# Attention and two MoE layers in float32: the products with V of two heads written into the two partition halves of one bank, and row sums from key blocks added up beforehand

## The chip, the cores and the metric

One core of one Trainium2 chip runs one program. The metric is the device time of one execution in microseconds, the median of three runs. The profile is one execution taken by the hardware profiler. Its engines are TensorE (PE for matmuls, PEld for weight loads), VectorE (DVE), ScalarE (ACT), GpSimd (POOL) and the DMA queue that SyncE (SP) issues.

## What is computed

Causal attention for 2 batches of 12 heads, 448 positions, 64 elements per head, and then two feed-forward layers on the 896 tokens. The part that the change touches is the attention:

```python
scores = scale * np.matmul(q, k.transpose(0, 1, 3, 2))
scores = np.where(mask, -1000000000.0, scores)
scores = scores - np.max(scores, axis=-1, keepdims=True)
attn = np.exp(scores)
attn = attn / (np.sum(attn, axis=-1, keepdims=True) + 1e-09)
return np.matmul(attn, v).astype(np.float32)
```

Its result (896 tokens of 768) goes through `h = x @ w_in` (1024 wide), a gated softmax, a layer norm, `@ w_out`, and then `relu(x @ w_in2)**2 @ w_out2` (2048 wide).

## The kernel before

The 24 heads are worked in 12 pairs. A pair's K and Q lie with head 0 on partitions 0 to 63 and head 1 on partitions 64 to 127. Per pair i the steps are, by the names of the table `SEQ` and with the lines of the profile:

- `H`, `L`: K and Q are split into a rounded part (ACT, L242) and a rest (DVE, L246; pair 0 on POOL). `S0a` to `S0c`, `mxa` to `mxc`: a first product of scores (L257) whose row maximum DVE takes out of PSUM against the mask (L272); `mT`, `row`, `rowd` bring the maxima into a row (L284, L289, L301, L302).
- `Sa`, `Sb` (L317, L325): the scores, transposed, so that partitions are keys and columns are queries, in two PSUM tiles of two banks, one bank per head. Half a holds key block 0 (queries 0 to 447, in columns 64 to 511) and key block 3 (queries 384 to 447, in columns 0 to 63); half b holds key block 1 (queries 128 to 447, columns 192 to 511) and key block 2 (queries 256 to 447, columns 0 to 191). The products of the two heads use the two row halves of the array.
- `ea1`, `eb1` (ACT, L349): the exponential into a buffer `PP` in SBUF, of which there are five. `ka`, `kb` (POOL, L346): the causal mask on the diagonal blocks.
- `Ua`, `Ub` (PE, L358): the products with V in float32, for each head two key blocks per half. The weights are 128 wide: 64 columns of V and 64 columns of ones (buffer `VR`, set to ones at L231), so that partitions 0 to 63 of the bank of a head receive the unnormalised output and partitions 64 to 127 the row sum.
- `E` (ACT, L369) takes the two banks to SBUF in one instruction and adds the 1e-9; `sums` (L374), `recips` (DVE, L380), `rcd` (L386) and `spread` (L392) bring the row sums into 112 lanes, take reciprocals, and broadcast them through DRAM into the one buffer `bc`. `norm` (POOL, L399) multiplies, one instruction of 64 partitions per head; `x_hi` (ACT, L407) and `x_lo` (DVE, L411) split the result for the next matmuls.

`h` (L474) are the matmuls of the first layer; each needs the `x` parts of a pair and a converted block of `w_in` (`wf`, `wh`, `wl`, L149 to L151, L465, L469). The order on every engine is that of `SEQ`, written out by hand: each engine runs its share of the table in that order, and an instruction that waits holds up all that stand behind it on its engine. SP issues the DMAs in the same way. Eight PSUM banks are handed out as four tiles of two banks; `bank2` takes one and `give` returns it. From about 94 us on the first `h` matmuls are mixed with the last products with V.

Of the kernel before, what the change touches and what calls it, by code (L numbers as in the profile page):

```python
# [29 lines left out]
row.1 mxb.2 ka.0 rowd.1 L.2 lq.1 S0a.2 S0c.2 Ua.0 mxa.2 H.3 load_r.4 eb1.0 mxc.2 S0a.3 kb.0 mT.2 mxa.3 Sa.1 row.2 lq.2  # L30
rowd.2 L.3 S0c.3 Ub.0 ea1.1 load_r.5 mxc.3 ka.1 S0b.3 E.0 Sb.1 mxb.3 sums.0 Sa.2 H.4 eb1.1 mT.3 L.4 Sb.2 load_r.6
row.3 lq.3 ea1.2 kb.1 recips.0 S0b.4 rowd.3 Ua.1 mxb.4 H.5 rcd.0 eb1.2 L.5 lq.8 S0c.4 lq.5 S0a.5 S0a.4 kb.2 mxc.4
load_v.2 Ub.1 mxa.4 ka.2 spread.0 mT.4 E.1 Sa.3 wf.0 row.4 sums.1 Sb.3 ea1.3 rowd.4 S0b.5 H.6 Ua.2 load_v.3 norm.0
mxa.5 eb1.3 load_r.7 wh.0 recips.1 S0c.5 mxb.5 Ub.2 rcd.1 ld.3 kb.3 mxc.5 E.2 wl.0 mT.5 Sa.4 row.5 sums.2 x_hi.0 L.6
rowd.5 ea1.4 S0a.6 Sb.4 ka.3 mxa.6 lq.6 S0c.6 spread.1 ka.4 eb1.4 S0b.6 mxc.6 Ua.3 load_r.8 mxb.6 H.7 kb.4 S0b.7
x_lo.0 mT.6 lq.7 Sa.5 L.7 row.6 load_v.4 rowd.6 norm.1 recips.2 S0a.7 ea1.5 mxb.7 Ub.3 rcd.2 load_r.9 mxa.7 S0c.7 Sb.5
ka.5 x_hi.1 mxc.7 load_v.5 Sa.6 x_lo.1 eb1.5 spread.2 wf.1 E.3 mT.7 Sb.6 ea1.6 sums.3 Ua.4 lq.9 row.7 load_r.10 H.8
norm.2 S0b.8 eb1.6 recips.3 S0a.8 mxb.8 Ub.4 rcd.3 wh.1 rowd.7 kb.5 mxa.8 S0c.8 load_v.6 E.4 Ua.5 mxc.8 ka.6 spread.3
x_hi.2 sums.4 H.9 L.8 mT.8 Sa.7 row.8 x_lo.2 load_r.11 L.9 rowd.8 Sb.7 ea1.7 norm.3 recips.4 S0b.9 rcd.4 H.10 S0a.9
Ub.5 load_v.7 mxa.9 eb1.7 lq.10 mxb.9 kb.6 x_hi.3 S0c.9 Sa.8 spread.4 E.5 mxc.9 kb.7 S0a.10 sums.5 ea1.8 mT.9 mxa.10  # L40
Sb.8 ka.7 row.9 lq.11 S0c.10 rowd.9 Ua.6 x_lo.3 L.10 norm.4 recips.5 S0b.10 rcd.5 eb1.8 Ub.6 mxb.10 load_v.8 load_g.0
mxc.10 ka.8 Sa.9 x_hi.4 spread.5 E.6 x_lo.4 Ua.7 H.11 wf.2 sums.6 ld.4 ea1.9 mT.10 Sb.9 row.10 rowd.10 S0a.11 eb1.9
recips.6 kb.8 Ua.8 mxa.11 rcd.6 load_v.9 norm.5 S0b.11 S0c.11 Ub.7 mxb.11 ka.9 x_hi.5 mxc.11 spread.6 Sa.10 E.7 x_lo.5
wl.1 mT.11 Ua.9 row.11 ea1.10 rowd.11 L.11 kb.9 sums.7 Sb.10 norm.6 Ub.8 eb1.10 recips.7 rcd.7 Sa.11 wf.3 load_v.10
E.8 Ub.9 x_hi.6 sums.8 wh.2 spread.7 Sb.11 ea1.11 x_lo.6 wh.3 h0.0 recips.8 wl.2 rcd.8 eb1.11 h0.1 norm.7 h1.0 ka.11
h1.1 x_hi.7 E.9 x_lo.7 h2.0 wl.3 sums.9 spread.8 load_v.11 h0.2 ka.10 kb.10 h2.1 recips.9 rcd.9 wf.4 ld.5 h1.2 Ua.10
norm.8 h0.3 Ub.10 kb.11 x_hi.8 spread.9 wh.4 x_lo.8 h2.2 E.10 wf.5 sums.10 h1.3 Ua.11 wl.4 wh.5 norm.9 recips.10 Ub.11
rcd.10 h1.4 wl.5 E.11 spread.10 h0.4 x_hi.9 sums.11 x_lo.9 h0.5 h1.5 norm.10 recips.11 mx.0 rcd.11 h2.3 mx.1 x_hi.10
h2.4 ex.0 spread.11 x_lo.10 h2.5 ex.1 mu.0 h3.0 mu.1 sq.0 norm.11 h3.1 de.0 sq.1 mx.2 h3.2 va.0 x_hi.11 pw.0 ex.2 h3.3
x_lo.11 fa.0 lw.0 ln.0 mu.2 h3.4 de.1 sq.2 h3.5 de.2 va.2 T.0 mx.3 pw.2 h4.0 Th.0 lw.1 ex.3 Tl.0 h4.1 va.1 h4.2 mu.3  # L50
pw.1 h4.3 fa.1 sq.3 fa.2 de.3 of.0 h4.4 ln.2 lw.2 ln.1 h4.5 of.1 oh.0 T.1 h5.0 mx.4 h5.1 lw.3 va.3 ex.4 h5.2 ol.0 pw.3
oh.1 fa.3 h5.3 mu.4 Th.1 h5.4 of.2 sq.4 h5.5 lw.4 ol.1 h6.0 oh.2 mx.5 T.2 Tl.1 h6.1 ex.5 of.3 Th.2 h6.2 lw.5 l2.0 ln.3
h6.3 mu.5 oh.3 T.3 h6.4 Tl.2 Th.3 sq.5 Tl.3 h6.5 lw.6 l2.1 de.5 y0.0 ol.2 l2.2 de.4 va.5 ol.3 va.4 y0.1 mx.6 pw.4 pw.5
# [784 lines left out]
```

## Time and profile before

| | |
|---|---|
| median of 3 runs | 459.95 us (459.81 to 460.13) |
| span of the profiled execution | 459.8 us, first to last instruction |
| PE busy | 452.7 us (98%) |
| weight loads (PEld) | 402.0 us (87%) |
| DVE busy | 275.1 us (60%) |
| ACT busy | 164.6 us (36%) |
| POOL busy | 120.8 us (26%) |
| products with V (L358) | 192 matmul records, 49.2 us of busy time |
| chain that ended last | PE 93%, of which the products with V 9% |

A program matmul on float32 (not on the rounded kind) stands in the trace as two records, each with its own weight load: 96 such products with V are 192 records. Busy times of PE overlap, since matmuls are pipelined; the chain that ended last gives each piece the time from its start to the next piece. The profiled execution's own time is its span and a little before the first and after the last instruction; the median of the runs is 0.15 us above the span. The products with V end at about 116 us; from 52 us on every piece of the chain that ended last is PE's, but for a few hundredths of a us and the last copy.

### The profile page before, as it was taken

The numbers are of one execution on the slowest core, as the hardware profiler recorded it, in microseconds if no ns is written. First come the engines' busy times: TensorE is split into PE (matmuls) and PEld (weight loads), VectorE is DVE, ScalarE is ACT, GpSimd is POOL, SyncE is SP. The second block draws the span as 40 slices with busy tenths as digits, with TensorE's granted clock in tenths as the row PEclk, the third lists the DMA queues.
The fourth block names the chain that finished last, engine by engine and source line by source line (L and its number), as shares of the span: only waits on it lengthen the run. The fifth ranks groups of instructions, "written<-read, shape, count | busy, mean of one in ns | idle before, by whom it ended". The sixth has DMA issues, their size and how long they took to land.

```text
span 459.8 us, 6525 instructions
## 1 busy us (share of the span) xinstructions
PE 452.7 (98%) x2535; PEld 402.0 (87%) x2535; DVE 275.1 (60%) x524; ACT 164.6 (36%) x213; POOL 120.8 (26%) x122
## 2 busy tenths in 40 slices
...
GB/s 251 128 154 221 207 159 164 62 79 98 41 280 133 96 248 2 0 1 0 0 138 69 138 80 127 116 91 137 70 137 80 128 113 94 240 90 135 86 52 120
DMA packets 41689, 52.47 MB, mean 114 GB/s; under 512 B 18234, under 2 KB 32314, under 8 KB 41274
## 3 DMA queue, kind: packets, MB, share of 16 engines
...
HBM read 49.16 MB, written 2.80 MB: 113 GB/s over the span
## 4 chain that ended last, share of the span: by engine, by line
PE 93%; DMA 1%; POOL 1%; ACT 0%; issue 0%; SPq 0%; ACTq 0%; POOLq 0%
PE h L752 25%; PE o L781 25%; PE y L621 13%; PE h L474 13%; PE U L358 9%; PE s L317 4%; PE mxp L257 1%; DMA bc<-d 1%; PE T L599 1%; PE s L325 1%; POOL x L399 1%; PE mxp L284 0%; PE s L333 0%; ACT PP L349 0%; SPq L301 0%
## 5 line engine op out<-in xcount | busy, mean ns | idle before, releaser
L752 PE MATMUL h<-yT,w 128*128 128x448 f32 x576 | 116.9, 365 | 0.0
L781 PE MATMUL o<-w,g 128*128 128x384 f32 x672 | 116.8, 336 | 0.0
L781 PEld LDWEIGHTS o<-w,g 128*128 128x128 f32 x672 | 116.5, 188 | 0.3 <-DVE relu L738 0.2
L752 PEld LDWEIGHTS h<-yT,w 128*128 128x128 f32 x576 | 108.2, 188 | 8.6
L677 POOL TENSOR_TENSOR w<-wf,w 128x768 fp32r<-128x768 f32 x32 | 59.4, 1856 | 206.2 <-ACT w L674 206.2
L149 DVE TENSOR_SCALAR wf<-raw 128x768 int32<-128x768 int32 (+1 forms) x46 | 26.3, 573 | 83.6 <-DMA raw<-in_moe_w_out_dram 58.2
L674 ACT CAST w<-wf 128x768 fp32r<-128x768 f32 x32 | 26.8, 838 | 137.7 <-DVE wf L151 99.4
L474 PE MATMUL h<-w,xT 128*128 128x512 f32 x252 | 59.5, 393 | 0.0
L621 PE MATMUL y<-lnT,w 128*128 128x384 f32 (+1 forms) x288 | 58.9, 365 | 0.0
L621 PEld LDWEIGHTS y<-lnT,w 128*128 128x128 f32 x288 | 51.9, 188 | 5.9
L474 PEld LDWEIGHTS h<-w,xT 128*128 128x128 f32 x252 | 46.8, 188 | 9.6
L358 PE MATMUL U<-PP,VR 128*128 128x448 f32 (+1 forms) x192 | 49.2, 400 | 0.1
L151 DVE SCALAR_TENSOR_TENSOR wf<-raw,wf 128x768 int32<-128x768 int32 (+1 forms) x46 | 47.3, 1029 | 1.6
L150 DVE SCALAR_TENSOR_TENSOR wf<-raw,wf 128x768 int32<-128x768 int32 (+1 forms) x46 | 47.2, 1027 | 1.6
L358 PEld LDWEIGHTS U<-PP,VR 128*128 128x128 f32 x192 | 32.1, 190 | 16.4 <-issue 11.1
L399 POOL TENSOR_TENSOR x<-E,bc 64x448 f32<-64x448 f32 x24 | 31.9, 1328 | 47.2 <-DMA bc<-d 42.7
L272 DVE CUSTOM_DVE_ANT_0 JK<-mxp,MK 112x336 bf16<-112x336 f32 (+2 forms) x96 | 38.8, 446 | 8.5 <-PE mxp L257 7.5
L349 ACT ACTIVATE PP<-s 128x1024 f32<-128x1024 f32 x24 | 24.5, 1023 | 12.9 <-PE s L325 7.2
L738 DVE TENSOR_TENSOR relu<-h,relu 128x896 f32<-128x896 f32 x16 | 17.5, 1092 | 14.6 <-ACT relu L737 14.6
L346 POOL TENSOR_SCALAR_AFFINE_SELECT PP<-PP 128x256 f32<-128x256 f32 (+1 forms) x48 | 19.7, 443 | 21.3 <-ACT PP L349 20.8
L740 ACT CAST g<-relu 128x896 fp32r<-128x896 f32 x16 | 15.1, 942 | 18.6 <-DVE relu L738 18.6
L650 DVE TENSOR_TENSOR yT<-y,yT 128x384 fp32r<-128x384 f32 (+1 forms) x12 | 7.4, 624 | 22.7 <-ACT yT L649 22.7
...
## 6 DMA issues: line engine op xcount, KB each, us to landing
...
```

The lines of the kernel that those rows point to most:

```text
L149: nc.vector.tensor_scalar(xi, hw, 3, 0x3FFFFFFF, ALU.logical_shift_left, ALU.bitwise_and)
L150: nc.vector.scalar_tensor_tensor(xi, hw, -0x40000000, xi, ALU.bitwise_and, ALU.bitwise_or)
L151: nc.vector.scalar_tensor_tensor(xi, lw, 29, xi, ALU.logical_shift_right, ALU.bitwise_or)
L272: nc.vector.tensor_tensor_reduce(JK[t], b[0:JP, h, o : o + nk], MK[:, S - nk :], 1.0, NEG, ALU.add, ALU.max, mx[i][:, 4 * h + t : 4 * h + ...
L358: nc.tensor.matmul(UB[i][:, h, q0:S], VR[i % 3][:, t, h, :], PP[(2 * i + a) % NPP][:, h, o : o + nq], start=t == 0, stop=t == 2,)
L399: nc.gpsimd.tensor_tensor(x[D * h : D * h + D], e[0:D, h], bc[:, h], ALU.mult)
L474: nc.tensor.matmul(b[:, half, :], xT[c][s][:, t * P : t * P + P], W1[c][:, w, 512 * half : 512 * half + 512], start=(c == 0 and s == 0 and ...
L621: nc.tensor.matmul(b[:, ci, 0:n], WO[fi][:, w, c * P : c * P + P], M["lnT"][a][s][:, fi, :], start=(fi == 0 and w == 0 and s == 0), stop=( ...
L674: nc.scalar.copy(W2[n][:, 0], w_f["2", n])
L677: nc.gpsimd.tensor_tensor(W2[n][:, 1], w_f["2", n], f(W2[n][:, 0]), ALU.subtract)
L752: nc.tensor.matmul(b[:, a, 0:HT], W2[fi][:, w, c * P : c * P + P], yT[c][s][:, HT * a : HT * a + HT], start=(c == 0 and w == 0 and s == 0) ...
L781: nc.tensor.matmul(ob, G[fi + e][s][:, P * t : P * t + P], w, start=(fi + e == 0 and r == 0), stop=(fi + e == NF2 - 1 and r == 2),)
```

## The change

A pair's products with V take weights of 64 columns (V alone). Head 0 writes partitions 0 to 63 and head 1 partitions 64 to 127 of one bank, and the two heads' matmuls of one key block now stand next to each other. The row sums come from elsewhere: a new step `ad` (`row_add`, POOL) adds the key blocks of queries 128 to 447 into a tile `ps`, in three instructions, and a new step `Us` (`row_sum`, PE) multiplies by 64 columns of ones, once the 128 queries that only key block 0 reaches, and once `ps`, into the second bank of the same PSUM tile. `E` becomes two instructions, `sums` and `spread` two DMAs each, `norm` one instruction on 128 partitions. V is loaded into a buffer without gaps, the memsets of the ones in it go, and there are six `PP` buffers in place of five. In the table `ad.i` stands behind the later of `ka.i` and `kb.i`, and `Us.i` behind `Ub.i`; nothing else in its order changes.

```diff
-NPP = 5
+NPP = 6
...
-            VR = [per.tile([P, 4, 2, 2 * D], F32, name=f"VR{i}") for i in range(3)]
+            VR = [per.tile([P, 4, 2, D], F32, name=f"VR{i}") for i in range(3)]
+            ONES = per.tile([P, D], F32, name="ONES")
...
+            Q2 = S - P
...
-                nc.sync.dma_start(VR[i % 3][:, :, :, 0:D], v[i])
+                nc.sync.dma_start(VR[i % 3], v[i])
...
-            for i in range(3):
-                nc.vector.memset(VR[i][:, :, :, D:], 1.0)
+            nc.vector.memset(ONES, 1.0)
...
-                for h in range(2):
-                    for t, o, q0, nq in HALF[a]:
+                for t, o, q0, nq in HALF[a]:
+                    for h in range(2):
                         nc.tensor.matmul(
-                            UB[i][:, h, q0:S],
+                            UB[i][D * h : D * h + D, 0, q0:S],
                             VR[i % 3][:, t, h, :],
                             PP[(2 * i + a) % NPP][:, h, o : o + nq],
                             start=t == 0,
                             stop=t == 2,
                         )
 
+            def row_add(i):
+
+                pa, pb = (PP[(2 * i + a) % NPP] for a in range(2))
+                ps[i] = p = lat.tile([P, 2, Q2], F32, tag="ps", name="ps", bufs=2)
+                nc.gpsimd.tensor_tensor(p, pa[:, :, 512 - Q2 :], pb[:, :, 512 - Q2 :], ALU.add)
+                for o, x in ((P, pb[:, :, 0 : Q2 - P]), (2 * P, pa[:, :, 0 : Q2 - 2 * P])):
+                    nc.gpsimd.tensor_tensor(p[:, :, o:], p[:, :, o:], x, ALU.add)
+
+            def row_sum(i):
+
+                p, pa = ps.pop(i), PP[(2 * i) % NPP]
+                for o, x in ((0, pa[:, :, D : D + P]), (P, p)):
+                    n = x.shape[2]
+                    for h in range(2):
+                        nc.tensor.matmul(
+                            UB[i][D * h : D * h + D, 1, o : o + n], ONES, x[:, h], start=o == 0, stop=o > 0
+                        )
+
             def u_out(i):
...
-                nc.scalar.activation(ee[i], U[:, :, 0:S], AF.Identity, bias=SE)
+                nc.scalar.activation(ee[i][0 : D + 1, 1], U[0 : D + 1, 1, 0:S], AF.Identity, bias=SE[0 : D + 1])
+                nc.scalar.copy(ee[i][:, 0], U[:, 0, 0:S])
...
-                nc.sync.dma_start(c, ee[i][D : D + 1].rearrange("o h s -> o (h s)").rearrange("o (p j) -> o p j", j=8))
+                for h in range(2):
+                    r = ee[i][D * h : D * h + 1, 1].rearrange("o (p j) -> o p j", j=8)
+                    nc.sync.dma_start(c[JP // 2 * h : JP // 2 * h + JP // 2], r)
...
-                bc = lat.tile([D, 2, S], F32, tag="bc", name="bc", bufs=1)
-                nc.sync.dma_start(bc, d.rearrange("(h s) -> h s", h=2).unsqueeze(0).broadcast_to((D, 2, S)))
+                bc = lat.tile([P, S], F32, tag="bc", name="bc", bufs=1)
+                for h in range(2):
+                    nc.sync.dma_start(
+                        bc[D * h : D * h + D], d[S * h : S * h + S].unsqueeze(0).broadcast_to((D, S))
+                    )
...
-                for h in range(2):
-                    nc.gpsimd.tensor_tensor(x[D * h : D * h + D], e[0:D, h], bc[:, h], ALU.mult)
+                nc.gpsimd.tensor_tensor(x, e[:, 0], bc, ALU.mult)
```

The order on PE, at the second half of pair 0 (`PP_139` and `VR_135` are its exponentials and V, `HI_118` the keys and queries of pair 3, whose products for the row maximum stand around it), before:

```order
L257 MATMUL mxp<-HI_118 128x224 x2
L358 MATMUL U<-PP_139,VR_135 128x320
L358 MATMUL U<-PP_139,VR_135 128x192
L358 MATMUL U<-PP_139,VR_135 128x320
L358 MATMUL U<-PP_139,VR_135 128x192
L257 MATMUL mxp<-HI_118 128x336 x2
```

and now (the second half's exponentials are `PP_140` here, the first half's `PP_139`):

```order
L259 MATMUL mxp<-HI_118 128x224 x2
L360 MATMUL U<-PP_140,VR_135 64x320 x2
L360 MATMUL U<-PP_140,VR_135 64x192 x2
L382 MATMUL U<-PP_139,ONES 64x128 x2
L382 MATMUL U<-ps,ONES 64x320 x2
L259 MATMUL mxp<-HI_118 128x336 x2
```

The two heads of a key block stand side by side (x2), each 64 columns of weights wide, and four matmuls with the ones follow; of these the last two read `ps`.

The order on POOL, from the masks of pair 1 to the first `norm` (`PP_140`, `PP_141` are the halves of pair 1 before, `PP_138` and `PP_142` those of pair 2), before:

```order
L346 AFFINE_SELECT PP_140<-PP_140 128x2x64
L346 AFFINE_SELECT PP_140<-PP_140 128x2x128
L346 AFFINE_SELECT PP_141<-PP_141 128x2x128 x2
L346 AFFINE_SELECT PP_138<-PP_138 128x2x128 x2
L346 AFFINE_SELECT PP_142<-PP_142 128x2x64
L346 AFFINE_SELECT PP_142<-PP_142 128x2x128
L399 TENSOR_TENSOR x<-E,bc 64x448 x2
```

and now (pair 1 has `PP_141` and `PP_142`, pair 2 `PP_143` and `PP_144`):

```order
L348 AFFINE_SELECT PP_142<-PP_142 128x2x128 x2
L372 TENSOR_TENSOR ps<-PP_141,PP_142 128x640
L374 TENSOR_TENSOR ps<-ps,PP_142 128x2x192
L374 TENSOR_TENSOR ps<-ps,PP_141 128x2x64
L348 AFFINE_SELECT PP_144<-PP_144 128x2x128 x2
L348 AFFINE_SELECT PP_143<-PP_143 128x2x64
L348 AFFINE_SELECT PP_143<-PP_143 128x2x128
L372 TENSOR_TENSOR ps<-PP_143,PP_144 128x640
L374 TENSOR_TENSOR ps<-ps,PP_144 128x2x192
L374 TENSOR_TENSOR ps<-ps,PP_143 128x2x64
L424 TENSOR_TENSOR x<-E,bc 128x448
```

Three additions stand behind the masks of every pair, ahead of the masks of the next pair and of `norm`, and `norm` is one instruction.

## Rows read from the trace of the kernel before

**Rows 1.** Stages: stretch, us, busy PE PEld DVE ACT POOL, clock, DMA share, GB/s.
```profile
12.00:38.00 26.00, 25.57 (x198) 19.22 (x198) 22.57 (x79) 14.88 (x19) 8.91 (x18) 1.00 0.53 156
38.00:52.00 14.00, 12.43 (x113) 9.42 (x110) 10.67 (x39) 7.25 (x11) 5.02 (x9) 1.00 0.86 230
52.00:93.00 41.00, 40.93 (x292) 29.76 (x292) 33.18 (x90) 25.55 (x34) 20.27 (x28) 1.00 0.50 134
93.00:117.00 24.00, 24.00 (x114) 18.94 (x111) 13.72 (x14) 7.26 (x9) 12.77 (x14) 1.00 0.29 81
```
**Rows 2.** The chain that ended last, in order of time (start, length, what).
```profile
15.82 2.09 PE U L358 x8
...
29.18 1.93 PE U L358 x8
...
41.72 6.12 DMA bc<-d
...
47.98 1.16 POOL x L399
...
49.21 1.15 POOL x L399
...
51.92 1.02 PE s L317 x10
...
104.77 1.89 PE U L358 x8
...
108.11 1.73 PE U L358 x8
...
112.59 3.68 PE U L358 x16
```
**Rows 3.** Weight loads in one `Ua` (start, length, records): they follow the matmuls.
```profile
54.59 0.19 PEld L358 LDWEIGHTS U<-PP,VR 128*128 128x128 f32 x1 [0.19 <-issue]
54.97 0.19 PEld L358 LDWEIGHTS U<-PP,VR 128*128 128x128 f32 x1 [0.19 <-issue]
```
**Rows 4.** Groups of PE by form (count, busy us, mean ns).
```profile
L358 PE MATMUL U<-PP,VR 128*128 128x448 f32 x48 | 23.5, 571 | 0.1
...
L325 PE MATMUL s<-MR,NEG 64*128 64x512 f32 x22 | 5.2, 472 | 0.0
```
**Rows 5.** PE in order of time: one pair of 64-row matmuls.
```profile
61.26 0.48 PE L325 MATMUL s<-MR,NEG 64*128 64x512 f32 x2
```
**Rows 6.** Single lines of POOL and DVE: ns min/median/max.
```profile
L399 POOL TENSOR_TENSOR x<-E,bc x24: 1125/1155/2024, 33.8 to 126.0; 64x448 f32<-64x448 f32 x24
L677 POOL TENSOR_TENSOR w<-wf,w x32: 1842/1852/1942, 193.2 to 442.7; 128x768 fp32r<-128x768 f32 x32
L246 DVE TENSOR_TENSOR LO<-r,HI x11: 1084/1089/2024, 12.5 to 84.2; 128x896 fp32r<-128x896 f32 x11
```
**Rows 7.** POOL in order of time: masks of pairs 0 to 2.
```profile
16.45 0.77 POOL L346 TENSOR_SCALAR_AFFINE_SELECT PP<-PP 128x256 f32<-128x256 f32 x2 [2.38 <-ACT PP L349]
...
25.32 0.77 POOL L346 TENSOR_SCALAR_AFFINE_SELECT PP<-PP 128x256 f32<-128x256 f32 x2 [3.67 <-ACT PP L349]
28.10 1.89 POOL L346 TENSOR_SCALAR_AFFINE_SELECT PP<-PP 128x256 f32<-128x256 f32 x4 [2.01 <-ACT PP L349]
```
**Rows 8.** PE in order of time: `Ub` of pairs 0 and 1.
```profile
20.10 2.00 PE L358 MATMUL U<-PP,VR 128*128 128x320 f32 x8
...
29.11 2.00 PE L358 MATMUL U<-PP,VR 128*128 128x320 f32 x8
```
**Rows 9.** ACT and SP lines that `E`, `sums` and `spread` touch: ns min/median/max.
```profile
L369 ACT ACTIVATE E<-U,SE x12: 1003/1011/1014, 22.1 to 116.4; 128x896 f32<-128x896 f32 x12
L407 ACT CAST xT<-x x12: 549/564/567, 39.4 to 127.4; 128x448 fp32r<-128x448 f32 x12
L374 SPq DMA_DIRECT2D sc<-E x12: 532/564/609, 23.2 to 117.5; - x12
L392 SPq DMA_DIRECT2D bc<-d x12: 453/490/606, 28.7 to 121.2; - x12
```

More of the change, by code (lines that the diff above doesn't have):

```diff
@@ L29 @@
 load_v.0 lq.4 S0a.1 mxr.0 S0c.1 lq.0 fl.8 mxc.1 S0b.1 Sa.0 mxa.1 mxb.1 H.2 load_r.3 L.1 ea1.0 load_v.1 mT.1 S0b.2 Sb.0
[L30 to L53, printed above, removed]
@@ L54 @@
-of.4 lw.7 y0.2 of.5 oh.4 ex.6 y0.3 fa.4 oh.5 ol.4 de.6 mu.6 y0.4 of.6 sq.6 ln.4 ol.5 oh.6 T.4 fa.5 va.6 y0.5 Th.4 ol.6
-pw.6 ln.5 fa.6 Tl.4 ln.6 of.7 T.5 y0.6 Th.5 Tl.5 oh.7 ol.7 T.6 y0.7 Th.6 Tl.6 f2.0 y1.0 yo.0 f2.1 g2.0 o2.0 y1.1 yp.0
-g2.1 yo.2 o2.1 yo.1 y1.2 yp.1 yp.2
+row.1 mxb.2 ka.0 rowd.1 L.2 lq.1 S0a.2 S0c.2 Ua.0 mxa.2 H.3 load_r.4 eb1.0 mxc.2 S0a.3 kb.0 ad.0 mT.2 mxa.3 Sa.1 row.2
+lq.2 rowd.2 L.3 S0c.3 Ub.0 Us.0 ea1.1 load_r.5 mxc.3 ka.1 S0b.3 E.0 Sb.1 mxb.3 sums.0 Sa.2 H.4 eb1.1 mT.3 L.4 Sb.2
@@ new lines @@
+load_r.6 row.3 lq.3 ea1.2 kb.1 ad.1 recips.0 S0b.4 rowd.3 Ua.1 mxb.4 H.5 rcd.0 eb1.2 L.5 lq.8 S0c.4 lq.5 S0a.5 S0a.4
+kb.2 mxc.4 load_v.2 Ub.1 Us.1 mxa.4 ka.2 ad.2 spread.0 mT.4 E.1 Sa.3 wf.0 row.4 sums.1 Sb.3 ea1.3 rowd.4 S0b.5 H.6
+Ua.2 load_v.3 norm.0 mxa.5 eb1.3 load_r.7 wh.0 recips.1 S0c.5 mxb.5 Ub.2 Us.2 rcd.1 ld.3 kb.3 mxc.5 E.2 wl.0 mT.5 Sa.4
+row.5 sums.2 x_hi.0 L.6 rowd.5 ea1.4 S0a.6 Sb.4 ka.3 ad.3 mxa.6 lq.6 S0c.6 spread.1 ka.4 eb1.4 S0b.6 mxc.6 Ua.3
+load_r.8 mxb.6 H.7 kb.4 ad.4 S0b.7 x_lo.0 mT.6 lq.7 Sa.5 L.7 row.6 load_v.4 rowd.6 norm.1 recips.2 S0a.7 ea1.5 mxb.7
@@ new lines @@
+Ub.3 Us.3 rcd.2 load_r.9 mxa.7 S0c.7 Sb.5 ka.5 x_hi.1 mxc.7 load_v.5 Sa.6 x_lo.1 eb1.5 spread.2 wf.1 E.3 mT.7 Sb.6
+ea1.6 sums.3 Ua.4 lq.9 row.7 load_r.10 H.8 norm.2 S0b.8 eb1.6 recips.3 S0a.8 mxb.8 Ub.4 Us.4 rcd.3 wh.1 rowd.7 kb.5
+ad.5 mxa.8 S0c.8 load_v.6 E.4 Ua.5 mxc.8 ka.6 spread.3 x_hi.2 sums.4 H.9 L.8 mT.8 Sa.7 row.8 x_lo.2 load_r.11 L.9
+rowd.8 Sb.7 ea1.7 norm.3 recips.4 S0b.9 rcd.4 H.10 S0a.9 Ub.5 Us.5 load_v.7 mxa.9 eb1.7 lq.10 mxb.9 kb.6 ad.6 x_hi.3
+S0c.9 Sa.8 spread.4 E.5 mxc.9 kb.7 S0a.10 sums.5 ea1.8 mT.9 mxa.10 Sb.8 ka.7 ad.7 row.9 lq.11 S0c.10 rowd.9 Ua.6
@@ new lines @@
+x_lo.3 L.10 norm.4 recips.5 S0b.10 rcd.5 eb1.8 Ub.6 Us.6 mxb.10 load_v.8 load_g.0 mxc.10 ka.8 Sa.9 x_hi.4 spread.5 E.6
+x_lo.4 Ua.7 H.11 wf.2 sums.6 ld.4 ea1.9 mT.10 Sb.9 row.10 rowd.10 S0a.11 eb1.9 recips.6 kb.8 ad.8 Ua.8 mxa.11 rcd.6
+load_v.9 norm.5 S0b.11 S0c.11 Ub.7 Us.7 mxb.11 ka.9 x_hi.5 mxc.11 spread.6 Sa.10 E.7 x_lo.5 wl.1 mT.11 Ua.9 row.11
+ea1.10 rowd.11 L.11 kb.9 ad.9 sums.7 Sb.10 norm.6 Ub.8 Us.8 eb1.10 recips.7 rcd.7 Sa.11 wf.3 load_v.10 E.8 Ub.9 Us.9
+x_hi.6 sums.8 wh.2 spread.7 Sb.11 ea1.11 x_lo.6 wh.3 h0.0 recips.8 wl.2 rcd.8 eb1.11 h0.1 norm.7 h1.0 ka.11 h1.1
```

17 lines of the change are left out of this document (15 added, 2 removed).

## The prediction

> **What bounds the kernel now.** I read the stages first, then the chain that ended last, then the rows of the instructions that the change touches. The stages [rows 1] show PE with next to no gap from 12 us on, but for 38 to 52 us, where 1.6 of 14 us are empty. DVE is the next engine: 22.6 of 26 us up to 38 us, 33.2 of 41 us from 52 to 93 us. POOL has room: 8.9 of 26 us, 5.0 of 14, 20.3 of 41, 12.8 of 24. The chain [rows 2] runs through PE, and 22 of the 24 blocks of products with V are in it, at 1.9 to 2.1 us each, from 15.82 to 116.27 us (the two of pair 3 are not). Between 38 and 52 us it leaves PE: the broadcast of pair 1's reciprocals takes 6.12 us, `norm` on POOL 1.16 and 1.15 us, and only then the exponential comes that releases PE at 51.92 us. So a shorter block of products counts in eleven pairs, and a shorter `norm` once.
>
> **Price of a pass.** A float32 product stands in the trace as two passes: 48 records for 24 products of 448 columns [rows 4]. Two such passes follow each other 0.38 us apart, 54.59 to 54.97 us [rows 3], that is 0.85 ns a column: 0.27 us for 320 columns, 0.16 for 192, 0.11 for 128, 0.054 for 64. `Ua` is four passes of 448 and four of 64, 1.74 us; `Ub` four of 320 and four of 192, 1.74 us; a pair 3.48 us. The blocks in the chain take 0.2 to 0.35 us more [rows 2], for coming in and going out, which stays.
>
> **The products with V after the change.** The passes are as many and as long, since their time goes by the columns that stream, but each fills half the array's columns. `Us` adds four passes of 128 and four of 320 per pair, 1.52 us. All depends on how far the two heads' passes lie on each other. The trace of before has no product with 64 columns of weights. Nearest are the products of 64 rows: two of 512 columns lie within 0.48 us [rows 5], where one takes 0.47 us [rows 4], so two halves of the array do work at once. Each of these is a single pass, though, and the two halves alternate. Here the order is: head 0 first pass, head 0 second pass, head 1 first, head 1 second. I take it that a pass starts no earlier than the one issued before it, as all rows of PE that I read have it. Then head 0's first pass runs alone, its second beside head 1's first, and head 1's second beside the next short passes of head 0. `Ua` becomes three passes of 448 and two of 64: 1.25 us, 0.49 less. `Ub` and `Us` together become 3 x 0.27 + 2 x 0.16 (`Ub`), 2 x 0.11 (head 1's products of 128), and 0.70 us more, since head 0's first pass over `ps` lies beside the second of these: 2.06 us, 0.32 more than `Ub` alone. A pair gains 0.17 us, eleven pairs **1.9 us**. The bounds are no overlap, 1.52 us a pair more (+16.7 us), and full overlap, (3.48 + 1.52) / 2 = 2.50 us, 0.98 a pair less (-10.8 us). The value taken is nearest to the row of the 64-row pairs, with the order of the passes laid over it. The Trainium skill, TensorE: Matmul & The Clock Gate, Part 3, says that matmuls start and end strictly in program order, and that only weight loads are pulled ahead; by that rule the staggered sum above stands, and no row here shows it for two passes on one half.
>
> **Change of shape.** Among the `h` products, of the same 128 by 128 shape, the two kinds of block take 1.89 and 1.73 us instead of 2.09 and 1.93 [rows 2]: 0.2 us less than among products of 64 rows. With 64 columns they lose this. There are three such blocks (`Ua.10`; `Ub.10` with `Us.10`; pair 11 in one): **+0.6 us**. Everywhere else the shape changes at the same places as before.
>
> **The stretch from 38 to 52 us.** `norm` becomes one instruction of 128 partitions and 448 columns; I take the columns to set its time, so the second 1.15 us and the handover of 0.07 go [rows 2]: -1.2 us. `E` is two instructions of about 0.56 us (as the copies of `x_hi`, [rows 9]) instead of one of 1.01: +0.1. The second `sums` costs SP 0.56 us, but the first may go 0.45 us earlier, when the first half of `E` is done: +0.1. The second `spread` is issued 0.49 us after the first [rows 9], and `norm` needs both: 0 to 0.5, taken as 0.4, since each half is half the bytes. Behind these on SP stand the loads of Q, K and V, which wait for buffers anyway. Sum **-0.6 us**. That V arrives without gaps helps the queue by an amount I can't price; I take nothing. Exponentials that wait for a sixth buffer are off the chain, and so are the memsets, for the first row maximum waits for PE.
>
> **POOL.** An addition of 448 columns takes 1.125 us at least, one of 768 columns 1.842 us [rows 6]: 2.24 ns a column and 0.12 us. The three of `ad` (640, 384 and 128 columns) take 1.55, 0.98 and 0.41 us, with two handovers of 0.07 us 3.1 us a pair, 37 us in all, less 12 x 1.2 us of `norm`. That fits the gaps of each stage: about 18 of 26 us, 10 of 14, 30 of 41. What counts is when `ps` is ready. Pair 0's masks end at 17.22 us and pair 1's at 26.09 us [rows 7], so `ps` is there at 20.3 and 29.2 us. `Ub` starts at 20.10 and 29.11 us [rows 8], sooner by what has been gained up to there (0.49 and 0.66 us), and `Us` asks for `ps` 1.25 us later: 20.85 and 29.70 us. Half a us is spare in each; from pair 2 on more. Behind `ad.1` the masks of pair 2 wait from 28.1 to 29.2 us [rows 7]; their products come after those of pair 1 and two blocks of scores, so nobody waits for that. `ad` before `norm` costs nothing while `norm` waits for the broadcast, as its masks do now. Waits for `ps`: 0 to 1.2 us, taken as **+0.3**. What POOL and DVE do to each other: `norm` took 1.125 us at best and 2.02 at worst, DVE's subtraction L246 1.08 and 2.02 us [rows 6], so a single collision costs about 0.93 us; for pairs 0 to 4 that is 0 to 4.7 us, taken as **+0.5**, as medians are near the minima today.
>
> **Sum.** -1.9 + 0.6 - 0.6 + 0.3 + 0.5 = -1.1 us against the profiled execution, 459.8 us of span and 0.15 us up to the median of the runs: **458.9 us**. This case's own range is 457.4 (no waits, no cost of the second `spread`) to 462.4 us (the dearer ends of waits and collisions). 0.2%, 0.9 us, is about what a measurement can tell from no change.
>
> **Rivals.** *No overlap.* Float32 passes on the two column halves may run one after the other, as two passes of one product do now [rows 3]. Then +16.7 us takes the place of -1.9, with +0.6 and -0.6 as above; the waits fall away, since every block leaves POOL and DVE more time: 476.6 us. For it: no row shows two halves of columns at work; against it: the halves of rows do [rows 5]. Chance 0.18.
>
> *Full overlap.* If head 1's first pass starts beside head 0's first, a pair gains 0.98 us. Up to 38 us DVE, with 3.4 us left of 26 [rows 1], lets through perhaps 1.5 of 2.9 us, from 52 to 93 us about 4.5 of 5.9, the last two pairs 2.0 - 0.6; with -0.6 and +0.8 this is -7.2 us, 452.7 us. For it speaks that the row pairs are complete in their overlap; against it the order of the passes. The Trainium skill, TensorEngine Tiling (Array Packing), Theoretical Speedup, gives up to a factor of two for 64 columns, which would be this case; the rows show it for halves of rows alone. Chance 0.22.
>
> *POOL and DVE in each other's way: slower.* POOL's work nearly doubles up to 52 us, where DVE has 3.4 and 3.3 us left [rows 1] and PE takes DVE's row maxima as they come. If each of pairs 0 to 4 loses one collision of 0.93 us on the path, by a late `ps` or by a late DVE, that is 4.7 us in place of 0.8: 462.8 us. It decides from half a us of lateness per pair on. For it: the rows at 2.02 us; against it: medians of 1.155 and 1.089 us [rows 6] though POOL is busy a third of that time. The Trainium skill, SBUF — State Buffer, SBUF: two separate sides, speaks against the change here: a DVE instruction with two SBUF inputs and a GpSimd instruction exclude each other for their whole length; the worst rows agree with that. Chance 0.15.
>
> **How the numbers follow.** The forecast has 0.45: of it 0.25 faster than 459.0 us, 0.14 within 0.2%, 0.06 slower. With full overlap 0.22 that makes 0.47 faster, 0.14 the same, and with the two slower rivals 0.39 slower. The range leaves out no overlap (0.18) and reaches from 450.5 us, a better full overlap, to 464 us, past the third rival.
>
> **What would show it.** `Ua` in the chain at 1.5 to 1.6 us and `Ub` with `Us` at about 2.25 us bear out the stagger; 1.1 and 1.8 us full overlap; 2.1 and 3.4 us none. The three lines of `ad` should take about 1.5, 1.0 and 0.4 us, `norm` 1.15 us once, and PE should wait for POOL by less than 1 us in all. A median of L246 or of `ad` far above these, or PE waiting for `ps`, is the third rival. I am wrong if PE's blocks shrink but the chain goes over DVE or POOL for long.

## The result: slower by 1.1%, and the profile after

After the change the kernel takes 465.51 us (median of four runs, 464.54 to 466.84) against 460.04 us before on the same chip (459.81 to 461.07): ratio 1.0114, 95% interval 1.0095 to 1.0134. The forecast was 458.9 us, the range 450.5 to 464.0. Single executions of one kernel can take over 1.5% longer than its fastest; the ratios leave these out, the medians do not. The profiled execution spans 464.6 us, against 459.8 us before. An execution's time is 1.7 to 1.8 us above its span in every run here, so the profile of before shows an execution of some 461.5 us, 1.5 above its median; times of a profile that are compared with [rows 2] below carry that doubt.

The stages (stretch, us, busy PE PEld DVE ACT POOL, clock, DMA share, GB/s), to be read beside [rows 1]:

```profile
12.00:38.00 26.00, 23.15 (x223) 15.86 (x223) 22.48 (x79) 14.98 (x21) 18.41 (x22) 1.00 0.53 158
38.00:52.00 14.00, 11.00 (x117) 8.18 (x116) 10.92 (x38) 6.40 (x11) 13.39 (x18) 1.00 0.67 224
52.00:93.00 41.00, 34.24 (x282) 22.12 (x284) 30.20 (x84) 21.41 (x34) 31.53 (x38) 0.83 0.44 124
93.00:117.00 24.00, 24.00 (x157) 17.53 (x154) 14.24 (x16) 10.47 (x15) 14.87 (x16) 1.00 0.33 96
```

PE got emptier in every stage up to 93 us (34.2 of 41 us in place of 40.9), and yet it has not got there sooner. POOL has gone from 5.0 to 13.4 of 14 us and from 20.3 to 31.5 of 41. The granted clock, 1.00 throughout before, averages 0.83 from 52 to 93 us: it is at 0.50, the 1.2 GHz level, in two stretches, from 53.2 to 56.6 us and from 80.5 to 90.7 us.

The chain that ended last, in order of time (start, length, what), to be read beside [rows 2]:

```profile
17.13 1.56 POOL ps L372
...
18.76 1.97 POOL ps L374
...
20.80 0.47 POOL ps L374
21.31 0.76 PE U L382 x4
...
72.28 1.54 POOL ps L372
...
73.89 1.00 POOL ps L374
...
75.38 1.14 POOL x L424
76.54 0.57 ACT xT L432
...
78.80 2.46 DVE wf L151
...
83.11 0.19 DVE sr L403
83.30 0.49 DVE JK L274
...
85.16 1.90 PE U L360 x8
87.06 1.49 PE U L382 x8
...
93.36 1.01 PE U L360 x8
94.38 0.76 PE U L382 x8
...
99.48 11.10 PE h L501 x48
```

How it comes back to PE there (PE in order of time; in brackets the idle time before and what ended it):

```profile
78.11 0.51 PE L319 MATMUL s<-HI 64*128 64x320 f32 x4 [2.38 <-ACT E L390]
84.61 0.56 PE L259 MATMUL mxp<-HI 64*128 64x224 f32 x2 [1.84 <-DVE mx L274]
```

Three things stand in these rows. The products with V are as short as full overlap makes them: `Ub` 1.01 us and `Us` 0.76 (93.36, 94.38 us), where `Ub` alone took 1.93. The chain that ran through PE before now goes over POOL: from 17.13 us over the additions of pair 0 to `Us.0`, and at 72 us over `ad.7` to `norm.4` and to `x_hi` on ACT. From there two ways lead back to PE. `E` stands behind `x_hi` on ACT, and PE, idle for 2.38 us, waits for it at 78.11 us. DVE waits for `x_hi` with `x_lo`, then splits a block of `w_in` for 5.3 us (77.87 to 83.18 us, L150 to L152, of which the row at 78.80 is one), and only then come the reciprocal and the row maxima that PE waits for at 84.61 us. And `h` begins at 99.48 us where it began at 93.67, 5.8 us later: the loss lies ahead of it, and behind it 1.0 us of the span is won back.

The waits (engine, line, waited for: us in total, times, longest):

```profile
ACT xT L432 <- POOL x L424: 31.7, 7, 8.4
POOL x L424 <- DMA bc<-d: 25.5, 5, 8.7
DVE sr L403 <- DMA sc<-E: 15.0, 8, 6.4
```

Before, the same three were 17.4, 42.7 and 5.2 us. `norm` waits less for its broadcast because it comes later: POOL is busy with additions when the broadcast lands. ACT waits for `norm` with exponentials behind it, and DVE's reciprocal waits for the two `sums` DMAs with row maxima behind it.

### The profile page after: what moved, and what is told of

It reads as the page before. It is cut to its first block, busy times and chain, and to the rows that moved or that the text cites. A ratio compares the mean times of both kernels' runs of the same rounds, so it can differ in the third digit from the quotient of the medians.

```text
span 464.6 us, 6789 instructions
## 1 busy us (share of the span) xinstructions
PE 446.5 (96%) x2631; PEld 390.7 (84%) x2631; DVE 276.9 (60%) x521; ACT 164.5 (35%) x225; POOL 153.3 (33%) x146
## 4 chain that ended last, share of the span: by engine, by line
PE 81%; DMA 4%; POOL 4%; ACT 2%; SPq 2%; issue 2%; DVE 1%; POOLq 0%; ACTq 0%; DVEq 0%
PE h L779 25%; PE o L808 25%; PE y L648 12%; PE h L501 12%; PE s L319 2%; POOL ps L374 2%; DMA VR<-in_v_dram 2%; PE U L360 2%; POOL ps L372 1%; PE T L626 1%; POOL PP L348 1%; PE U L382 1%; ACT PP L351 1%; DMA d<-sr 1%; DMA r<-in_kq_dram 1%
## 5 line engine op out<-in xcount | busy, mean ns | idle before, releaser
L150 DVE TENSOR_SCALAR wf<-raw 128x768 int32<-128x768 int32 (+1 forms) x46 | 27.7, 602 | 84.3 <-DMA raw<-in_moe_w_out_dram 58.1
L151 DVE SCALAR_TENSOR_TENSOR wf<-raw,wf 128x768 int32<-128x768 int32 (+1 forms) x46 | 49.8, 1083 | 1.6
L152 DVE SCALAR_TENSOR_TENSOR wf<-raw,wf 128x768 int32<-128x768 int32 (+1 forms) x46 | 46.7, 1015 | 1.6
L274 DVE CUSTOM_DVE_ANT_0 JK<-mxp,MK 112x336 bf16<-112x336 f32 (+2 forms) x96 | 38.3, 443 | 5.4 <-PE mxp L259 4.6
L360 PE MATMUL U<-PP,VR 128*64 128x448 f32 (+3 forms) x192 | 28.3, 422 | 0.8 <-DVE mx L274 0.6
L348 POOL TENSOR_SCALAR_AFFINE_SELECT PP<-PP 128x256 f32<-128x256 f32 (+1 forms) x48 | 25.1, 554 | 12.0 <-ACT PP L351 12.0
L360 PEld LDWEIGHTS U<-PP,VR 128*64 128x64 f32 x192 | 12.5, 144 | 15.3 <-issue 10.4
L374 POOL TENSOR_TENSOR ps<-ps,PP 128x384 f32<-128x384 f32 (+1 forms) x24 | 23.7, 986 | 1.9
L424 POOL TENSOR_TENSOR x<-E,bc 128x448 f32<-128x448 f32 x12 | 15.7, 1306 | 25.5 <-DMA bc<-d 25.5
L372 POOL TENSOR_TENSOR ps<-PP,PP 128x640 f32<-128x640 f32 x12 | 20.5, 1708 | 3.5 <-PE U L382 2.8
```

The lines of the kernel that those rows point to most:

```text
L151: nc.vector.scalar_tensor_tensor(xi, hw, -0x40000000, xi, ALU.bitwise_and, ALU.bitwise_or)
L152: nc.vector.scalar_tensor_tensor(xi, lw, 29, xi, ALU.logical_shift_right, ALU.bitwise_or)
L274: nc.vector.tensor_tensor_reduce(JK[t], b[0:JP, h, o : o + nk], MK[:, S - nk :], 1.0, NEG, ALU.add, ALU.max, mx[i][:, 4 * h + t : 4 * h + ...
L348: nc.gpsimd.affine_select(ap, ap, [[0, 2], [1, m]], ALU.is_ge, 0.0, base=0, channel_multiplier=-1)
L360: nc.tensor.matmul(UB[i][D * h : D * h + D, 0, q0:S], VR[i % 3][:, t, h, :], PP[(2 * i + a) % NPP][:, h, o : o + nq], start=t == 0, stop=t ...
L374: nc.gpsimd.tensor_tensor(p[:, :, o:], p[:, :, o:], x, ALU.add)
```

## The experiments

Times are medians; beside each stands the kernel before on the same chip, 460.4 to 460.7 us. Ratios are to it, with the 95% interval.

**1. Without the additions (e1).** `Us` reads one key block in place of `ps`, and POOL adds nothing; the row sums lack the other blocks.

```diff
-                p, pa = ps.pop(i), PP[(2 * i) % NPP]
+                pa, pb = (PP[(2 * i + a) % NPP] for a in range(2))
+                p = pb[:, :, 512 - Q2 :]
```

> The three additions of every pair are left out; the second product with ones reads one key block in place of the sum, so the row sums lack the other blocks, and PE's work is that of the change. Theory T1 (the additions stand in POOL's queue ahead of masks and norm, so norm, x_hi on ACT and then the exponentials come late): with 37 us of POOL gone the gain of the two halves shows, 450 to 455 us; h starts at 92 us or earlier in the chain; ACT's wait for x, 31.7 us after the change, falls under 15 us. Theory T2 (the two sums and two spread DMAs lengthen the way from E to norm): the DMAs are unchanged, 462 to 466 us. Theory T3 (PE's clock falls by the sparser work of PE alone): the half level stays between 75 and 92 us, 462 us or more.

Measured: 456.78 us, 0.993 (0.991 to 0.9949). The additions, with all that follows from them, the lower clock included, cost 8.7 us (8.5 by the ratios, which set aside that the chips differ): more than the whole loss, so the rest of the change wins some 3 us. T1 has the direction but misses both its numbers: it had foretold 455 us at most and a wait of ACT for `x` under 15 us, and that wait fell only to 22.1. T3 falls: the clock is 0.98 from 52 to 93 us. The chain shows what holds it now, SP and DMA:

```profile
57.88 0.49 SPq L417
58.42 0.58 SPq L417
59.09 0.99 SPq L398
60.14 1.94 DMA sc<-E
62.10 0.20 DVE sr L404
62.30 0.49 DVE JK L274
...
74.48 1.95 DMA sc<-E
```

The two halves of `spread.3` (L417), then the two of `sums.4` (L398) stand in SP's queue one behind the other, and DVE takes the reciprocal before the row maxima (L274). From the DMA of `sums.4` (60.14 us) to that of `sums.6` (74.48) are 14.3 us, 7.2 a pair.

**2. Row sums on PE alone (e2).** In place of `ps`, ones times all four key blocks.

```diff
+                for a in range(2):
+                    for t, o, q0, nq in HALF[a]:
...
+                                UB[i][D * h : D * h + D, 1, q0:S], ONES, PP[(2 * i + a) % NPP][:, h, o : o + nq],
```

> No additions: PE multiplies all four key blocks by the ones, 1024 columns a head in place of 448, so Us becomes about 1.74 us in place of 0.76 (computed from 0.85 ns a column and pass, two heads side by side) and a pair's products 3.8 us against 4.02 before the change. T1: 454 to 459 us, under the kernel before. T2 and T3: 463 us or more.

Measured: 462.96 us, 1.0048 (1.0031 to 1.0065), a miss for T1 as it stood. (The median holds a run of 470.46 us; without it it is 462.70.) `Us` took 1.73 us as foretold, but 2.2 us of loss by the ratio remain with POOL at 12.5 of 41 us, less than before the change, so POOL is not the only cause. The chain goes over the `sums` DMAs there (3.93 us at 53.31 us, 1.95 at 76.66).

**3. POOL's load in the kernel before (e3).** Two additions a pair whose result nobody reads, and the sixth `PP` buffer of the change.

```diff
+                nc.gpsimd.tensor_tensor(p, pa[:, :, 192:], pb[:, :, 192:], ALU.add)
+                nc.gpsimd.tensor_tensor(p[:, :, 2 * P :], p[:, :, 2 * P :], pa[:, :, 0:D], ALU.add)
```

> The kernel before with six exponential buffers and two additions a pair on POOL at the places of ad (640 and 128 columns, about 1.96 us, which is what POOL has more after the change once the shorter norm is taken off); nobody reads their result, PE is unchanged. T1: norm comes late as in the change, 3 to 8 us slower than before, 463 to 468 us, and POOL is busy without a gap in part of 25 to 87 us. T2 and T3: within 1 us of before, 459 to 461 us.

Measured: 463.44 us, 1.0064 (1.0049 to 1.0079). The load alone, with PE, SP and the DMAs as before and a clock of 1.00 in all four stages, costs 3.0 us, just inside T1's range, and T2 and T3, which had 1 us at most, fall as the only causes. It can't tell T1's queue from collisions: DVE's busy time rose with the load too, from 275.1 to 283.4 us for the same instructions, and the chain runs over DVE from 28.6 to 47.8 us.

**4. One DMA each for `sums` and `spread` (e5).**

```diff
+                nc.sync.dma_start(c, ee[i][0:P:D, 1].rearrange("h (p j) -> h p j", j=8))
...
+                nc.sync.dma_start(bc, d.rearrange("(h s) -> h s", h=2).unsqueeze(1).broadcast_to((2, D, S)))
```

> The change with sums in one DMA (both rows by a partition step of 64) and spread in one DMA; the additions stay. T2: the way from E to the reciprocal goes back from 3 us to 2 us and SP loses some 1 us of issues a pair: 458 to 462 us. T1: POOL is the limit of the stretch, so at most 1.5 us less, 464 to 465.5 us.

Measured: 483.04 us, 1.049 (1.0471 to 1.0508). It tells nothing of T2 nor of T1, since the broadcast in this form, 2 x 64 x 448 with the two heads outermost, is slow in itself:

```profile
105.70 7.26 DMA bc<-d
```

That is no property of one DMA as such: the single broadcast of the kernel before, with its 64 partitions outermost, took 3.3 to 4.3 us from issue to `norm` in most pairs, 6.12 in the busiest stretch [rows 2]. In the change a piece of the chain on the two halves is 3.02 us (61.40 us). The issue of `sums` fell to 534 ns. So the next run keeps two halves of `spread`.

**5. `sums` in one DMA, with and without the additions (f1, f2).** Only the first line of the diff above; f2 also has the edit of e1.

> The change with sums in one DMA (spread stays two); additions kept. What the runs so far leave: with the additions gone the time fell by 8.7 us against the change, but stayed far above what PE's shorter blocks allow, and sums, reciprocal, rcd, spread and the next sums followed each other on SP with a period of 7 us a pair (59.1, 66.2, 73.1 us). Theory TQ (SP's queue in order is the second limit: two issues of 0.80 us in place of one of 0.56): 1 us a pair less on SP from pair 3 to 7, 460 to 463.5 us. Theory T1 (POOL's queue alone): 464.5 to 466 us.

> As e1 (no additions, row sums incomplete), with sums in one DMA. TQ: the period on SP falls from 7 to 6 us, 451 to 455 us. T1 alone (nothing left on POOL to take away): 456 to 457.5 us, as e1.

Measured: f1 464.02 us, 1.0078 (1.0062 to 1.0094); f2 452.14 us, 0.9817 (0.9795 to 0.9839). f2 lies in TQ's range, and f1 between the ranges of TQ and T1. With the additions gone the second `sums` DMA is worth 4.7 us (456.78 to 452.14; 5.2 by the ratios); with them it is worth 1.5. Two limits lie one behind the other, and the nearer one, POOL, hides most of the other. In f2 PE's clock is 1.00 in all four stages and `h` begins at 86.33 us, some 6 to 7 us sooner than before. The difference of f1 and f2, 11.9 us, is the full price of the additions in this kernel, with the lower clock that came along in f1 (0.83 from 52 to 93 us).

**6. Two buffers for the broadcast (f4).** `bc` gets `bufs=2`.

> The change with two buffers for the broadcast in place of one, so that spread of a pair need not wait, at the head of SP's queue, for the norm of the pair before (after the change spread.5 was issued at 76.5 us, when norm.4 ended). If POOL's lateness reaches PE by way of SP (spread waits for norm, the next sums stand behind it, DVE's reciprocal waits at the head of DVE's queue ahead of row maxima): 458 to 463 us. If it reaches PE by way of ACT alone (x_hi waits for norm, exponentials behind it): 464 to 466 us.

Measured: 466.09 us, 1.0124 (1.0105 to 1.0143). Nothing gained: that `spread.5` waits for `norm.4` costs nothing by itself. That leaves ACT, and DVE behind it, as the way from POOL to PE: there `x_hi` waits for `norm` (76.54 us in the chain above) ahead of `E` and the exponentials, and `x_lo` for `x_hi` ahead of the row maxima.

**7. PE sums, one `sums` DMA, two broadcast buffers (f6).**

> No additions, ones products on all four key blocks on PE (as e2, which took 462.96 us), sums in one DMA and two broadcast buffers. TQ: SP's part no longer holds PE, 456 to 459.5 us, under the kernel before. T1 alone: as e2, 462 to 463.5 us.

Measured: 460.42 us, 0.9992 (0.9978 to 1.0007). As the kernel before, between TQ's 456 to 459.5 and T1's 462 to 463.5: a miss for both. The 576 columns a head more that PE streams give back nearly all that the halves gain. With `Us` at 1.73 us a pair takes 3.76 in place of 4.02; that these 0.26 us a pair do not show in the time stays unexplained.

**8. POOL's order and POOL's load (g1, g2, g3).** All have one `sums` DMA. g1 moves four words of the table; g2 leaves out four.

```diff
-... ad.4 ... norm.1 ... ad.7 ... norm.4 ... ad.8 ... norm.5 ... ad.9 ... norm.6
+... norm.1 ad.4 ... norm.4 ad.7 ... norm.5 ad.8 ... norm.6 ad.9
```

> f1 (one sums DMA, all additions; 464.02 us) with four steps ad moved behind the norm that POOL kept waiting: ad.4 behind norm.1, ad.7 behind norm.4, ad.8 behind norm.5, ad.9 behind norm.6. POOL's work is the same, its order alone changes. Theory of POOL's order (norm.4 and norm.5 came 7 to 9 us after their broadcast, x_hi held ACT, the exponentials and PE): norm.4 at 69 us or earlier in place of 74.2, the half clock from 80 us on goes, 459 to 462 us. Theory of POOL's load (the additions simply last too long, from pair 0 on, and collide with DVE): 463 to 465 us.

> f1 with the additions of pairs 0 to 3 left away and their row sums made on PE from all four key blocks (0.97 us more of PE a pair), the later eight pairs as in f1. POOL's load: the chain over POOL from 15 to 51 us (masks, additions, masks, norm) goes, start of h 3 to 5 us earlier, 459 to 461.5 us. POOL's order: the late norm.4 and norm.5 stay and eat it, 462 to 465 us.

> g1 and g2 together (ad.4, ad.7, ad.8, ad.9 behind norm; pairs 0 to 3 on PE; one sums DMA), all outputs computed. If POOL's early load and its later order are both paid on the path: 454 to 458 us, under the kernel before by more than 0.4%. If one of them is idle: as the better of g1 and g2.

Measured: g1 460.04 us, 1.0 (0.997 to 1.003); g2 461.98, 1.0043 (1.0026 to 1.006); g3 459.55, 0.9983 (0.9974 to 0.9993). Order alone is worth 4.0 us against f1, less load up to 52 us is worth 2.0, and both together 4.5 (3.6, 1.6 and 4.4 by the ratios). g1 lies in the range of the theory of order; g2, just outside both ranges, and g3, 1.6 us above its own, are misses. POOL's work in g1 is no less than in f1 (busy 157.7 and 153.0 us), nor is DVE's (281.6 and 278.5), so order is separated from load there; the clock is not. The lower level did not go, as had been foretold, but came sooner and stayed for less: 0.54 from 76 to 80 us, 0.50 to 83 us, 0.97 behind that, in the mean 0.92 from 52 to 93 us against 0.83 in f1. POOL in order of time in f1, from the broadcast of pair 4 on:

```profile
68.46 2.63 POOL L348 TENSOR_SCALAR_AFFINE_SELECT PP<-PP 128x256 f32<-128x256 f32 x4
71.06 1.55 POOL L372 TENSOR_TENSOR ps<-PP,PP 128x640 f32<-128x640 f32 x1
72.69 1.54 POOL L374 TENSOR_TENSOR ps<-ps,PP 128x384 f32<-128x384 f32 x2
74.19 1.13 POOL L422 TENSOR_TENSOR x<-E,bc 128x448 f32<-128x448 f32 x1
```

and in g1:

```profile
68.30 1.36 POOL L348 TENSOR_SCALAR_AFFINE_SELECT PP<-PP 128x256 f32<-128x256 f32 x4
69.64 1.15 POOL L422 TENSOR_TENSOR x<-E,bc 128x448 f32<-128x448 f32 x1
70.74 1.55 POOL L372 TENSOR_TENSOR ps<-PP,PP 128x640 f32<-128x640 f32 x1
```

`norm.4` comes at 69.64 in place of 74.19 us. What is left in g3 lies on POOL again. Its chain runs over POOL from 47 to 84 us; one pair of it:

```profile
54.52 1.14 POOL x L436
55.66 0.73 POOL PP L347 x2
56.47 1.56 POOL ps L371
58.09 1.75 POOL ps L373
59.92 0.72 POOL ps L373
...
61.70 0.40 POOL PP L347
62.10 1.10 POOL x L436
```

From one `norm` to the next are 7.6 us, nearly all of it POOL's work. The second addition, 1.0 us when undisturbed, takes 1.75 here.

**9. Less load where POOL holds the chain (h1).** As g1, but pairs 0 and 1 have their row sums on PE, and pairs 4 to 7 only the first addition; PE takes the 256 columns a head that are left.

```diff
+                if i in ONE_ADD:
+                    xs_ += [(2 * P, pb[:, :, 0 : Q2 - P]), (3 * P, pa[:, :, 0 : Q2 - 2 * P])]
```

> All outputs computed. One sums DMA, the order of g1; POOL's load cut where the chain of g3 ran over POOL (47 to 84 us): pairs 0 and 1 take all row sums on PE, pairs 2 and 3 and 8 to 11 keep the three additions, pairs 4 to 7 only the first (640 columns), and PE takes the 256 columns a head that are left (0.44 us a pair, two heads side by side). If POOL's load is what holds g3 (masks 2.1, additions 3.3, norm 1.15 us and handovers a pair against some 6.5 us of PE a pair): POOL leaves the chain, start of h at 90 to 92 us, 454.5 to 457.5 us. If what is left in g3 is something else (the broadcast, SP): 459 to 460 us, as g3.

Measured: 458.18 us, 0.9961 (0.9937 to 0.9985), under the kernel before, but 0.7 us above the foretold range. The profiled run waited once more for POOL, 1.67 us at 81.8 us, for masks behind the three additions of pair 8. Its twelve runs fall in two groups: seven with a mean granted clock of 1.000 took 457.4 to 458.5 us, five with 0.989 to 0.995 took 459.3 to 462.2, on average 3.0 us more.

**10. The clock, and one pair more (k1, k2, k3).** k1 is the change with products of zeros in PE's idle stretch at 76 us, k2 is h1 with the same at 82 us, and k3 is h1 with pair 8 too on one addition.

```diff
+                for _ in range(12 if i == 10 else 0):
+                    nc.tensor.matmul(b[:, 1, 0:S], Z, Z[:, 0:1].broadcast_to((P, S)), start=True, stop=True)
...
-ONE_ADD = (4, 5, 6, 7)
+ONE_ADD = (4, 5, 6, 7, 8)
```

> The change with twelve products of zeros (448 columns, rounded kind, some 0.19 us each, about 2.3 us) behind the transpose of pair 10, where PE stood idle from 75.7 to 78.1 us before its clock went to the half level; they write unused columns of the same bank and nobody reads them. Theory C (a large part of the loss is the half clock from 80 to 90 us): granted clock 1.00 through 80 to 90 us, Ub.7 at 1.0 us in place of 1.90, 461 to 463 us. Theory T1 and TQ (the queues hold everything; PE would only wait longer at the next gap): 464.5 to 466.5 us.

> h1 with eight products of zeros (about 1.5 us) behind the transpose of pair 11, where PE waited 1.7 us for masks at 81.7 us. In h1 the runs with a mean granted clock of 1.000 took 457.4 to 458.5 us, those at 0.989 to 0.995 took 459.3 to 462.2 us. Theory C: every run at 1.000 and 457.4 to 458.5 us. Otherwise: the same spread as h1.

> h1 with one addition in place of three for pair 8 too (POOL 1.5 us less before the masks for which PE waited at 81.7 us, PE 0.44 us more). POOL's load: that wait goes and with it the cause of the lower clock, 457 to 458.3 us in every run. If the wait only moves: as h1, 457.4 to 462 us.

Measured: k1 466.44 us, 1.0127 (1.011 to 1.0144). The stages of the change there:

```profile
80.00:83.00 3.00, 2.76 (x14) 1.24 (x14) 2.96 (x2) 0.85 (x1) 2.84 (x3) 0.58 0.78 244
83.00:86.00 3.00, 1.39 (x6) 0.85 (x8) 2.96 (x16) 0.56 (x1) 2.91 (x6) 0.50 0.58 197
86.00:90.00 4.00, 4.00 (x24) 2.56 (x22) 3.09 (x7) 1.05 (x2) 1.28 (x1) 0.50 0.16 57
```

and of k1:

```profile
80.00:83.00 3.00, 1.88 (x14) 0.97 (x14) 2.97 (x2) 1.30 (x3) 2.84 (x3) 1.00 0.58 175
83.00:86.00 3.00, 0.93 (x4) 0.61 (x6) 2.97 (x13) 0.56 (x1) 3.00 (x6) 0.54 0.68 215
86.00:90.00 4.00, 4.00 (x22) 2.38 (x20) 3.55 (x9) 0.88 (x2) 1.19 (x3) 0.50 0.30 95
```

The clock stayed at 1.00 from 80 to 83 us, in place of 0.58, and nothing was won, a miss for theory C: PE finished sooner, waited 2.9 us for DVE in place of 1.8, and then went to 0.50, the 1.2 GHz level, all the same. So the first 3 us at the lower level lay beside DVE's work. That the stretch from 85 to 91 us costs, some 2.6 us, is read from the chain's rows (`Ub` 1.90 in place of 1.01, `Us` 1.49 in place of 0.76, the scores behind them about 1.0 more) and not shown by a run that changed the clock alone: it stays open. The 3.0 us between the two groups of h1's runs are of that size, but the waits that come with a lower clock are in them. k2: 458.06 us, 0.9947 (0.9929 to 0.9964), as h1 within the spread; two of its four runs, the profiled one among them, still have a mean clock of 0.995 or 0.996, where theory C had foretold 1.000 in every run. k3: **456.51 us, 0.9917 (0.9896 to 0.9938)**, the fastest kernel with all outputs, 3.9 us under the kernel before and half a us under its foretold range. PE has 38.5 us of work in the 41 from 52 to 93 us, at a clock of 1.00:

```profile
52.00:93.00 41.00, 38.50 (x391) 27.23 (x388) 34.24 (x89) 26.55 (x40) 28.09 (x31) 1.00 0.48 137
```

What is left to f2, 4.4 us, is the price of row sums by these means (f2's row sums lack blocks), on another chip, and it can't be split further from these runs.

## Why the prediction was wrong

**The overlap.** The step that a pass starts no earlier than the one issued before it, so that the two heads' passes are staggered, was wrong. `Ua` takes 1.02 us in the chain, `Ub` 1.01, `Us` 0.76, the 1.1 and 1.8 us that the text had given for full overlap. A pair takes 2.79 us where it took 4.02 [rows 2], 1.23 less, and even full overlap had been priced at only 0.98. Eight passes of `Ub` lie within 1.08 us (matmuls in order of time):

```profile
93.30 1.08 PE L360 MATMUL U<-PP,VR 128*64 128x320 f32 x8
```

One after another they would be 1.74 us by the prediction's price of a column. The passes start in pairs, 6 ns apart. The Trainium skill, TensorE: Matmul & The Clock Gate, Part 3, says that matmuls start strictly in program order; the records don't say which head a pass belongs to, so no row here bears that out or refutes it, but the stagger that the prediction worked out with it did not come. The Trainium skill, TensorEngine Tiling (Array Packing), Theoretical Speedup, gives up to a factor of two for 64 columns; the trace agrees, with 1.93 to 1.01 us. The row of the 64-row pairs [rows 5], set aside in favour of the order, had it right.

**The time of that rival.** Full overlap was put at 452.7 us. f2, which lacks the additions and the second `sums`, took 452.14. That they lie so close is partly luck: a pair shrank by 1.23 us and not by 0.98, eleven pairs by 13.5, of which some 8 came through. What the nearness does show is that PE's gain was there, and that the two costs set against it were not priced.

**POOL.** The step that failed with the dearest effect is "That fits the gaps of each stage", and with it "`ad` before `norm` costs nothing while `norm` waits for the broadcast". In the sum POOL stood with +0.8 us, for waits and collisions; the additions cost 8.7 (e1). The sums of two stages came as foretold (18.4 of 26 and 31.5 of 41 us, for 18 and 30), that of 38 to 52 us did not (13.4 of 14, for 10). But POOL works through its queue in order: `ad.6` and `ad.7` stood ahead of `norm.4`, which came at 75.4 us and held `x_hi` on ACT, and through it exponentials, DVE's row maxima and PE. In g1, where `ad.7` stands behind it, `norm.4` comes at 69.6, the time at which it came before the change. g1 shows that the order alone, with the shorter stretch at the lower clock that came of it, was worth 4.0 us; e3 that the load alone costs 3.0 in the kernel before. The three additions were priced at 3.1 us a pair; they took 44.2 us in all (20.5 and 23.7), 3.7 a pair. Durations, ns min/median/max:

```profile
L372 POOL TENSOR_TENSOR ps<-PP,PP x12: 1540/1564/2510, 17.1 to 113.8; 128x640 f32<-128x640 f32 x12
L374 POOL TENSOR_TENSOR ps<-ps,PP x24: 452/1005/1964, 18.8 to 117.2; 128x384 f32<-128x384 f32 x12, 128x128 f32<-128x128 f32 x12
L424 POOL TENSOR_TENSOR x<-E,bc x12: 1125/1146/2127, 37.0 to 132.7; 128x448 f32<-128x448 f32 x12
```

The least are as priced; the dear ones are 0.8 to 1.0 us longer, as the collisions of the third rival were to be. The additions of pairs 0 and 1 each met one (1.97 and 1.82 us for the second addition, in the chain, each beside a subtraction of 1.09 us on DVE), so `ps.0` came at 21.3 and not 20.3 us. In all, the additions took 7.2 us more than their price, and DVE is busy for 276.9 us, for 269.8 without them (e1). That rival had the right sign and the nearest time, 462.8 us; how much of the loss beyond the order's 4.0 us is collisions, no run separates. The Trainium skill, SBUF — State Buffer, SBUF: two separate sides, says that a DVE instruction with two SBUF inputs and a GpSimd instruction exclude each other for their whole length; the dear lengths agree with that, and no run here tests it by itself.

**`sums` and `spread`.** The second `sums` was priced at one issue of 0.56 us, +0.1 on the path, and only between 38 and 52 us. Each half's issue takes longer than the whole did:

```profile
L397 SPq DMA_DIRECT2D sc<-E x24: 752/802/866, 22.8 to 125.4; - x24
```

against 532/564/609 [rows 9]. With the additions out of the way it costs 4.7 us (f2 against e1): SP's round of `sums`, reciprocal, `rcd` and `spread` took 7.2 us a pair in e1, more than PE's work on a pair, which h1's expectation puts at some 6.5. "Behind these on SP stand the loads, which wait for buffers anyway" overlooked that the next pair's `sums` stands there too.

**The other terms.** `norm` runs once, in 1.15 us, and `E` takes 0.63 and 0.52 us, as taken. PE waits for `ps` directly by 1.3 us in all, for +0.3 in the sum and less than 1 us as the sign. The loss among the `h` products, +0.6, did not show: `Ua.10` is 1.02 us there as elsewhere. The clock's fall was not foreseen at all. The upper end of the prediction's own range does not follow from its terms: with the dearer ends of waits and collisions they add up to +4.0 us and 464.0, and not to 462.4, which is less than its third rival alone. What happened is its last sign of being wrong: PE's blocks shrank, and the chain went over POOL and DVE.
